# Regrouping the attention segments of a memory-augmented block: 20 tiles of three and 2 of two instead of 21 of three and one of one

## Chip, cores, metric

One core of a Trainium2 chip. The metric is the device time of one execution in microseconds (us). Most executions of one kernel agree within 0.3%, which here is about as large as the effect under study; the finer readings are therefore taken from traces, between fixed points of the program.

## The reference, cut to what matters

The output is `x + A(xn) + B(xn)` with `xn = layernorm(x)`, for 2048 tokens of width 1024. `B` is a mixer followed by an MLP. `A` cuts the tokens into 64 segments of 32, puts 8 memory rows before each, and runs attention with 32 heads of size 128 over the 40 rows. A segment's memory is the attention output at the memory rows of the segment before:

```
for s in range(n_seg):
    h = concat([mem, xs], axis=1)           # 8 memory rows, 32 tokens
    q, k, v = h @ Wq, h @ Wk, h @ Wv        # 32 heads of 128
    scores = where(mask, q @ k.T * scale, -1e9)
    o = softmax(scores) @ v @ Wo
    mem = o[:, :M]                          # memory of the next segment
    outs.append(o[:, M:])
```

## The kernel before

The kernel replaces the serial chain of memories by a closed form that it checks at the end (with a serial fallback that does not run here), so all segments can be computed at once. Each segment then needs 33 columns, 32 tokens and one memory column; the first tile has 7 more. Segments are packed into tiles, at most three to a tile, which is 99 rows of at most 128; a mask keeps the segments of a tile apart. Tiles are packed into five blocks. For each block and each group of four heads, the kernel projects the block's columns to Q and K (64 matmuls, whose moving operand is as wide as the block), then for each tile does four score matmuls, a softmax, a transpose by DMA, and four value matmuls. 64 = 21 x 3 + 1, so one tile held a single segment:

```python
def tiles_of(b):
    gis = list(range(4 * b, 4 * b + 4)) + ([21] if b == 3 else [20] if b == 4 else [])
    ...
        s = 1 if gi == 21 else 3            # segments in the tile
    ...
```

Blocks 0 to 4 had 4, 4, 4, 5 and 5 tiles and 403, 396, 396, 429 and 495 columns. The projection reads its columns as one run in blocks 0 and 3 ("flat"), and in blocks 1, 2 and 4 as strips of 99, each starting at a multiple of 104:

```python
if b == 3:
    rhs = lambda k: hTb[:, k, :nb]
else:
    rhs = lambda k: hTb[:, k, :].rearrange("p (t c) -> p t c", t=nt)[:, :, 0:99]
...
for k in range(KT):     # 8 matmuls, one PSUM bank
    nc.tensor.matmul(ps[:, :nb] ..., w[:, k, hh * P:(hh + 1) * P], B["rhs"](k), start=(k == 0), stop=(k == KT - 1))
```

The groups of a tile of T columns, for a group of four heads; the first operand of a matmul after the output is the stationary one, loaded as weights:

```python
for hh in range(4):     # scores: stationary 128 x T, moving 128 x T
    nc.tensor.matmul(S3[:, hh, :], QT[:, hh, c0:c0 + T], KTt[:, hh, c0:c0 + T], start=True, stop=True)
...                     # mask, exp, sum, scale, transpose
for hh in range(4):     # values: stationary T x 128, moving T x T
    nc.tensor.matmul(O3[:, hh, :], V[:T, t["i"], hh * P:(hh + 1) * P], PTr[:T, hh, :T], start=True, stop=True)
```

The score and value groups are issued between projections of eight matmuls each, so that TensorE always has work.

Of the kernel before, what the change touches and what calls it, by code (L numbers as in the profile page):

```python
# [15 lines left out]
BF16 = mybir.dt.bfloat16  # L16
# [7 lines left out]
P = 128  # L24
S = 2048
D = 1024
KT = D // P
# [3 lines left out]
H = 32  # L31
DH = 128
M = 8
SEG = 32
# [43 lines left out]
def kernel(  # L78
# [16 lines left out]
    nc = tc.nc  # L95
# [14 lines left out]
    R1_v = R1_d.rearrange("(n p) d -> p n d", p=P)  # L110
    xn_d = tc.dram_tile([S, D], BF16, name="xn_scratch")
    xn_v = xn_d.rearrange("(n p) d -> p n d", p=P)
    hT_d = {b: tc.dram_tile([P, KT * c], BF16, name=f"hT{b}_scratch") for b, c in ((1, 416), (2, 416), (3, 432), (4, 520))}
    V_d = tc.dram_tile([S, H * DH], BF16, name="V_scratch")
    Vr_d = tc.dram_tile([NQ + 1, H * DH], BF16, name="Vmem_scratch")

# [17 lines left out]
    eye9 = const_tile("c_eye9", np.concatenate([np.eye(M, dtype=np.float32), np.ones((M, 1), np.float32)], 1))  # L134
    mask_first = const_tile("c_mask_first", _tile_mask(3, True))
    mask_reg = const_tile("c_mask_reg", _tile_mask(3, False))
    mask_last = const_tile("c_mask_last", _tile_mask(1, False))
    GT = cpool.tile([P, KT, NQ], F32)
    MZ = cpool.tile([P, KT, NQ + 1], BF16)
    gthr = cpool.tile([1, NQ], F32)  # L140
# [15 lines left out]
    def row_norms(pool, ppool, tag, src, in_place=False):  # L156
# [6 lines left out]
        nc.tensor.matmul(ps[:1, :NQ], ones_f[:], sr[:], start=True, stop=True)  # L163
        return ps

    def tiles_of(b):
        gis = list(range(4 * b, 4 * b + 4)) + ([21] if b == 3 else [20] if b == 4 else [])
        out_, c = [], 0
        for i, gi in enumerate(gis):
            s = 1 if gi == 21 else 3  # L170
            first = b == 0 and i == 0
            nm = s + (M - 1 if first else 0)
            msk = mask_first if first else (mask_reg if s == 3 else mask_last)
            r0 = 0 if first else 7 + 3 * gi
            out_.append(dict(c0=c, ntok=s * SEG, nm=nm, T=s * SEG + nm, mask=msk, r0=r0, tok=i * 96, i=i, gi=gi))
            c += s * SEG + nm
        return out_, c

    def fill(hTb, tl, x_of):

        for t in tl:
            a = 96 * t["gi"]
            end = a + t["ntok"]
            while a < end:
                j, o = divmod(a, P)
                w = min(P - o, end - a)
                d = t["c0"] + a - 96 * t["gi"]
                nc.vector.tensor_copy(hTb[:, :, d:d + w], x_of(j)[:, :, o:o + w])
                a += w
            d = t["c0"] + t["ntok"]  # L190
            nc.vector.tensor_copy(hTb[:, :, d:d + t["nm"]], MZ[:, :, t["r0"]:t["r0"] + t["nm"]])

    with tc.manual_schedule(engines={mybir.EngineType.PE, mybir.EngineType.SP, mybir.EngineType.Pool}), ExitStack() as actx:
# [6 lines left out]
        with ExitStack() as bctx:  # L200
# [381 lines left out]
            for hg in range(8):  # L582
                cs_ = slice(hg * 512, (hg + 1) * 512)
                while len(wvs) < min(8, hg + 3):
                    load_wv()
                wv = wvs[hg]
                if 1 <= hg < 5:
                    nc.gpsimd.dma_start(wo_sb[:, (hg - 1) * 8:hg * 8, :], Wo_v[:, (hg - 1) * 8:hg * 8, :])
                for m4 in range(4):
                    Vs = vsp.tile([P, 4, 512], BF16, tag="Vs")  # L590
                    for j in range(4):
                        ps = psum.tile([P, 512], F32, tag="mm", bufs=4)
                        for k in range(KT):
                            nc.tensor.matmul(ps[:], xT[:, m4 * 4 + j, k, :], wv[:, k, :], start=(k == 0), stop=(k == KT - 1))  # L594
                        if j % 2 == 0:
                            nc.scalar.copy(Vs[:, j, :], ps[:])  # L596
                            if (hg, m4, j) == (7, 3, 2):
                                nc.scalar.activation(etab[:], ps[:, 0:1], ACTF.Exp, scale=0.0)
                        else:
                            nc.vector.tensor_copy(Vs[:, j, :], ps[:])  # L600
                    nc.sync.dma_start(V_d[m4 * 512:(m4 + 1) * 512, cs_].rearrange("(j p) c -> p j c", p=P), Vs[:])
                if hg == 1:
                    for t in pns:
                        nc.gpsimd.memset(t[:], 0.0)
                if 1 <= hg < 5:
                    b, (tl, nb) = hg, tiles_of(hg)
                    if b != 3:
                        for t in tl:
                            t["c0"] = 104 * t["i"]
                    hTs = abig.tile([P, KT, 432 if b == 3 else 104 * len(tl)], BF16, tag="oX", name=f"hTs{b}")  # L610
                    nc.gpsimd.memset(hTs[:], 0.0)
                    fill(hTs, tl, lambda j, b=b: xT[:, j])
                    nc.gpsimd.dma_start(hT_d[b][:], hTs[:].rearrange("p k c -> p (k c)"))
                if hg == 6:
                    first_w = [wtile(), wtile()]
                    for w, src in zip(first_w, (Wq_v, Wk_v)):
                        nc.sync.dma_start(w[:], src[:, :, 0:512])
                if hg == 7:
                    second_w = [wtile(), abig.tile([P, KT, 512], BF16, tag="oXb", name="wk1")]
                    for w, src in zip(second_w, (Wq_v, Wk_v)):  # L620
                        nc.sync.dma_start(w[:], src[:, :, 512:1024])
                if hg == 0:
                    tl, nb = tiles_of(0)
                    hTb0 = early.tile([P, KT, 408], BF16, tag="hTb0")
                    fill(hTb0, tl, lambda j: xT[:, j])
# [7 lines left out]
        def block_setup(b):  # L633
            tl, nb = tiles_of(b)
            ntok = sum(t["ntok"] for t in tl)
            if b == 0:
                hTb, rhs = hTb0, lambda k: hTb0[:, k, :nb]
            else:
                nt = len(tl)
                hTb = early.tile([P, KT, 432 if b == 3 else 104 * nt], BF16, tag=f"hTb{b % 2}")  # L640
                nc.gpsimd.dma_start(hTb[:].rearrange("p k c -> p (k c)"), hT_d[b][:])
                if b == 3:
                    rhs = lambda k: hTb[:, k, :nb]
                else:
                    rhs = lambda k: hTb[:, k, :].rearrange("p (t c) -> p t c", t=nt)[:, :, 0:99]
                    for t in tl:
                        t["c0"] = 104 * t["i"]
            return dict(b=b, tiles=tl, nb=nb, ntok=ntok, rhs=rhs, cols=nb if b in (0, 3) else 104 * len(tl))

        def load_values(B, V, hg):  # L650
            b, cs_ = B["b"], slice(hg * 512, (hg + 1) * 512)
            r, n = 384 * b, 5 if b == 4 else 4
            nc.sync.dma_start(V[0:96, 0:n, :], V_d[r:r + 96 * n, cs_].rearrange("(t p) c -> p t c", p=96))
            if b == 0:
                nc.sync.dma_start(V[96:106, 0, :], Vr_d[0:10, cs_])
                nc.sync.dma_start(V[96:99, 1:4, :], Vr_d[10:19, cs_].rearrange("(t j) c -> j t c", j=3))
            else:
                nc.sync.dma_start(V[96:99, 0:n, :], Vr_d[7 + 12 * b:7 + 12 * b + 3 * n, cs_].rearrange("(t j) c -> j t c", j=3))
            if b == 3:
                nc.sync.dma_start(V[0:32, 4, :], V_d[S - 32:S, cs_])  # L660
                nc.sync.dma_start(V[32:33, 4, :], Vr_d[70:71, cs_])

        def proj(B, w, hh, dst, scale):
            nb, nt = B["nb"], len(B["tiles"])
            flat = B["b"] in (0, 3)
            ps = psum.tile([P, 512], F32, tag="mm", bufs=4)
            for k in range(KT):
                nc.tensor.matmul(ps[:, :nb] if flat else ps[:, :nb].rearrange("p (t c) -> p t c", t=nt), w[:, k, hh * P:(hh + 1) * P], B["rhs"](k), start=(k == 0), stop=(k == KT - 1))  # L668
            if flat:
                o, i = dst[:, hh, :nb], ps[:, :nb]  # L670
            else:
                o, i = dst[:, hh, :].rearrange("p (t c) -> p t c", t=nt)[:, :, 0:99], ps[:, :nb].rearrange("p (t c) -> p t c", t=nt)
            if scale is None:
                nc.scalar.copy(o, i)  # L674
            else:
                nc.scalar.mul(o, i, scale)  # L676
# [37 lines left out]
        class Out:  # L714
# [4 lines left out]
            def piece(self, hg):  # L719
# [3 lines left out]
                    self.Rt = iop.tile([P, 512], F32, tag="Rt")  # L723
                    nc.gpsimd.dma_start(self.Rt[:, :self.w], R_v[:, self.gi, self.cc])
                for h in range(4 * hg, 4 * hg + 4):
                    nc.tensor.matmul(self.ps[:, :self.w], self.oX[self.gl // 3][:, h, self.gl % 3 * P:(self.gl % 3 + 1) * P], wo_sb[:, h, self.cc], start=(h == 0), stop=(h == H - 1))  # L726
                if hg == 7:
                    ot = iop.tile([P, 512], BF16, tag="ot")
                    if DEBUG_A:
# [45 lines left out]
        for gi_, group in enumerate(groups):  # L775
# [3 lines left out]
            for hg in range(8):  # L779
# [26 lines left out]
                for i, (B, t, QT, KTt, V) in enumerate(work):  # L806
                    due = clock[0] + 1.0 + i * step
                    if B["b"] not in oXs:
# [1 line left out]
                        if B["b"] == 3:  # L810
                            oXs[3].append(abig.tile([P, H, P], BF16, tag="oXb", name="oXb"))
                        oX_last = oXs[B["b"]]
                    j, at = divmod(480 if t["gi"] == 21 else t["tok"], 384)
                    oX = oXs[B["b"]][j]

                    def s_item(t=t, hg=hg, QT=QT, KTt=KTt, V=V, oX=oX, at=at, due=due, gi_=gi_):
                        PTr = scores(t, hg, QT, KTt)
# [4 lines left out]
                        smalls.append((clock[0] + (12.0 if gi_ == 0 else 10.0), ("O", gi_), o_item))  # L822
                        return 0.18
                    smalls.append((due, ("S", gi_), s_item))
            outs = [Out(oXs[B["b"]], 3 * B["b"] + gl, gl, ch * 512) for B in Bs for gl in range(4 if B["b"] == 4 else 3) for ch in range(2)]


        o = outs.pop()
# [184 lines left out]
```

## Time and profile before

| | before |
|---|---|
| median time | 1520.25 us (3 runs, 1520.1 to 1525.81) |
| span of the profiled run | 1518.8 us |
| TensorE (PE) busy | 99% |
| VectorE / ScalarE busy in blocks 3 and 4 | 47% / 46% |
| blocks 1 and 2 / blocks 3 and 4, from the trace | 278.04 us / 314.75 us |

The last row is measured between starts on PE: from the first row that the timeline labels with the width of block 1 (the eight matmuls before it are merged into a row of block 0) to the first projection of block 3, and from there to what follows the last projection of block 4.

From the page of the kernel before: busy time by engine, the granted clock in 40 slices, and the chain that ended last, by engine.

```profile
PE 1508.2 (99%) x9778; PEld 806.7 (53%) x9850; DVE 545.9 (36%) x1138; ACT 504.8 (33%) x1142; POOL 179.1 (12%) x248
...
PEclk9999999999999999999999999999999999999999
...
PE 97%; DMA 1%; issue 0%; ACT 0%; SPq 0%; DVE 0%
```

PE is busy, at full clock, and it is the chain. A busy PE is not a PE at its peak: matmuls overlap in the trace. So durations say little, and the spacing from one start to the next says what a group costs. The next view, who PE waited for (us in total, times, longest), shows that there is nothing to win from waits.

```profile
PE warm L334 <- DVE wz L328: 1.4, 1, 1.4
PE psO L707 <- DMA PT<-Pn: 0.4, 1, 0.4
...
PE ps L307 <- DMA w_sb<-in_B_w_dram: 0.3, 1, 0.3
PE pso L726 <- issue: 0.2, 1, 0.2
```

The last row is no wait: at that place four weight loads stand on record but only three matmuls, so one matmul record is missing. Waits shorter than the view lists can still be read from starts: at 1291.26 us, in block 4, a value group starts 0.11 us late.

Timeline of the kernel before, in block 3, around a score group of the one-segment tile. The columns are start in us, duration in us, engine (PE matmuls, PEld weight loads), line, operation, operands, count.

```profile
1227.08 1.62 PE L668 MATMUL ps<-hTb,wt 128*128 128x429 bf16 x8
1228.62 0.16 PEld L683 LDWEIGHTS <-QT 128*33 128x33 bf16 x4 [0.36 <-issue]
1228.62 0.27 PE L683 MATMUL psS<-KT,QT 128*33 128x33 bf16 x4
...
1228.82 1.20 PEld L668 LDWEIGHTS <-wt 128*128 128x128 bf16 x8
1228.82 1.63 PE L668 MATMUL ps<-hTb,wt 128*128 128x429 bf16 x8
1230.11 0.40 PEld L683 LDWEIGHTS <-QT 128*99 128x99 bf16 x4
1230.29 0.35 PE L683 MATMUL psS<-KT,QT 128*99 128x99 bf16 x4
```

Read it by starts. The first projection takes 1228.62 - 1227.08 = 1.54 us before the 33-wide group can start; one ahead of a 99-wide group takes 1230.29 - 1228.82 = 1.47 even here, and 1.45 elsewhere. The 33-wide group takes 0.20 us, more than the 0.187 of a 99-wide one that streams three times as many columns. The weight loads of the 99-wide group start 0.18 us ahead of its first matmul (1230.11 to 1230.29); those of the 33-wide group start with it, and so do those of the projection behind it (1228.82). So there is a loss at both ends. In the single starts, the first 33-wide matmul comes 0.09 us late and the first of the projection behind the group 0.08 us late.

Timeline of the kernel before: a run of 16 flat 429-column matmuls, a run of 16 in five strips of 99, and what follows each.

```profile
1208.63 3.07 PE L668 MATMUL ps<-hTb,wt 128*128 128x429 bf16 x16
1211.54 0.35 PE L683 MATMUL psS<-KT,QT 128*99 128x99 bf16 x4
...
1364.25 3.54 PE L668 MATMUL ps<-hTb,wt 128*128 128x495 bf16 x16
1367.63 0.35 PE L683 MATMUL psS<-KT,QT 128*99 128x99 bf16 x4
```

The spacing is 2.91/16 = 182 ns and 3.38/16 = 211 ns (typically 3.37). In this trace 512 columns take 216 ns and 128 take 56, so 384 more columns take 160 ns, which is 2.4 columns per ns. At that rate 429 and 495 columns are 178.8 and 206.3 ns, so the five strips of 99 carry a little more on top than the flat run does.

### The profile page before, as it was taken

The numbers are of one execution on the slowest core, as the hardware profiler recorded it, in microseconds if no ns is written. First come the engines' busy times: TensorE is split into PE (matmuls) and PEld (weight loads), VectorE is DVE, ScalarE is ACT, GpSimd is POOL, SyncE is SP. The second block draws the span as 40 slices with busy tenths as digits, with TensorE's granted clock in tenths as the row PEclk, the third lists the DMA queues.
The fourth block names the chain that finished last, engine by engine and source line by source line (L and its number), as shares of the span: only waits on it lengthen the run. The fifth ranks groups of instructions, "written<-read, shape, count | busy, mean of one in ns | idle before, by whom it ended". The sixth has DMA issues, their size and how long they took to land.

```text
span 1518.8 us, 24267 instructions
## 1 busy us (share of the span) xinstructions
PE 1508.2 (99%) x9778; PEld 806.7 (53%) x9850; DVE 545.9 (36%) x1138; ACT 504.8 (33%) x1142; POOL 179.1 (12%) x248
## 2 busy tenths in 40 slices
PE   9999999999999999999999999999999999999998
PEld 7844444445444444444466645654665555445555
DVE  8382230100110122212146614651663266416542
ACT  6533203013022011111256614650663266326630
POOL 5231020211111231100000010001000100010001
PEclk9999999999999999999999999999999999999999
DMA  8699762353355887532499948992997399728711
GB/s 287 153 272 318 217 177 91 133 201 112 125 169 145 194 284 254 189 133 70 139 239 253 239 117 188 247 238 81 227 239 189 119 223 203 197 76 208 175 45 54
DMA packets 303387, 274.20 MB, mean 181 GB/s; under 512 B 153787, under 2 KB 270032, under 8 KB 303016
## 3 DMA queue, kind: packets, MB, share of 16 engines
q1 hardware_dynamic: 281096, 189.92, 49.5%
q0 software_dynamic: 22032, 82.63, 15.8%
q8 instruction: 79, 1.29, 0.4%
q14 instruction: 36, 0.29, 0.1%
q10 hardware_dynamic: 144, 0.07, 0.0%
HBM read 190.98 MB, written 46.19 MB: 156 GB/s over the span
## 4 chain that ended last, share of the span: by engine, by line
PE 97%; DMA 1%; issue 0%; ACT 0%; SPq 0%; DVE 0%
PE ps L668 30%; PE pso L726 14%; PE ps L594 14%; PE ps L536 13%; PE ps L562 13%; PE ps L394 4%; PE ps L317 3%; PE psS L683 2%; PE psO L707 2%; PE ps L486 1%; PE ps L853 1%; DMA w_sb<-in_B_w_dram 1%; PE gps L465 0%; PE ps L451 0%; DMA wt<-in_A_Wq_dram 0%; DMA PT<-Pn 0%
## 5 line engine op out<-in xcount | busy, mean ns | idle before, releaser
L668 PE MATMUL ps<-hTb,wt 128*128 128x396 bf16 (+3 forms) x2528 | 500.4, 344 | 0.1
L668 PEld LDWEIGHTS <-wt 128*128 128x128 bf16 x2528 | 231.9, 97 | 167.6 <-DMA wt<-in_A_Wq_dram 0.5
L594 PE MATMUL ps<-wt,xT 128*128 128x512 bf16 x1003 | 220.1, 379 | 1.1
L726 PE MATMUL pso<-wo_sb,oX 128*128 128x512 bf16 x938 | 209.3, 379 | 1.2 <-issue 0.2
L536 PE MATMUL ps<-xn3T,w_sb 128*128 128x512 bf16 x896 | 196.2, 379 | 0.0
L562 PE MATMUL ps<-w_sb,h3T 128*128 128x512 bf16 x873 | 194.3, 379 | 1.2
L594 PEld LDWEIGHTS <-xT 128*128 128x128 bf16 x1024 | 100.0, 98 | 121.0
L537 ACT ACTIVATE h3T<-ps 128x512 bf16<-128x512 f32 x112 | 66.8, 597 | 290.4 <-PE ps L536 289.5
L726 PEld LDWEIGHTS <-oX 128*128 128x128 bf16 x960 | 92.5, 98 | 108.4
L674 ACT CAST KT<-ps 128x396 bf16<-128x396 f32 (+3 forms) x160 | 82.1, 513 | 186.9 <-PE ps L668 185.9
L562 PEld LDWEIGHTS <-h3T 128*128 128x128 bf16 x896 | 86.8, 98 | 103.5
L536 PEld LDWEIGHTS <-w_sb 128*128 128x128 bf16 x896 | 86.4, 98 | 102.3
L689 DVE TENSOR_REDUCE sums<-sm 99x4 f32<-99x396 f32 (+2 forms) x176 | 97.5, 554 | 113.7 <-ACT sm L687 113.7
L676 ACT ACTIVATE QT<-ps 128x396 bf16<-128x396 f32 (+3 forms) x160 | 84.1, 525 | 118.7 <-PE ps L668 102.8
L685 DVE TENSOR_TENSOR sm<-psS,c_mask_reg_sb 99x396 f32<-99x396 f32 x160 | 91.2, 570 | 85.3 <-PE psS L683 84.7
L596 ACT CAST Vs<-ps 128x512 bf16<-128x512 f32 x64 | 37.4, 585 | 233.2 <-PE ps L594 175.0
L687 ACT ACTIVATE sm<-sm 99x396 f32<-99x396 f32 (+2 forms) x176 | 92.7, 527 | 64.6 <-DVE sm L685 61.0
L600 DVE CAST Vs<-ps 128x512 bf16<-128x512 f32 x64 | 44.2, 691 | 170.1 <-PE ps L594 158.1
L695 DVE TENSOR_TENSOR Pn<-sm,rs 99x396 bf16<-99x396 f32 (+2 forms) x176 | 98.9, 562 | 8.2 <-DMA PT<-Pn 2.1
L563 DVE TENSOR_TENSOR R<-ps,R 128x512 f32<-128x512 f32 x32 | 22.0, 690 | 182.7 <-PE ps L562 173.4
L733 POOL DMA_DIRECT2D out_dram<-ot x30 | 16.3, 545 | 584.0 <-DVE ot L732 578.1
L732 DVE TENSOR_TENSOR ot<-pso,Rt 128x512 bf16<-128x512 f32 (+1 forms) x33 | 22.3, 675 | 172.1 <-PE pso L726 166.9
(124 smaller groups left out, 1068.9 us busy)
## 6 DMA issues: line engine op xcount, KB each, us to landing
wt<-in_A_Wq_dram SPq DMA_DIRECT2D x76, 512.0 KB
wt<-in_A_Wk_dram SPq DMA_DIRECT2D x76, 512.0 KB
wt<-in_A_Wv_dram POOLq DMA_DIRECT2D x24, 1024.0 KB, 6.5
V_scratch<-Vs SPq DMA_DIRECT2D x32, 512.0 KB
V<-V_scratch SPq DMA_DIRECT2D x32, 384.0 KB
R_scratch<-x POOLq DMA_DIRECT2D x16, 512.0 KB, 3.8
R<-R_scratch SPq DMA_DIRECT2D x16, 512.0 KB
R_scratch<-R POOLq DMA_DIRECT2D x16, 512.0 KB, 3.1
```

The lines of the kernel that those rows point to most:

```text
L536: nc.tensor.matmul(ps[:].rearrange("p (n t) -> p n t", t=P), w3_sb[:, k, f * P:(f + 1) * P], xn3T[tb][:, :, k, :], start=(k == 0), stop=(k ...
L537: nc.scalar.activation(h3T[:, f, :], ps[:], ACTF.Gelu_apprx_tanh)
L562: nc.tensor.matmul(ps[:], h3T[:, f, j * P:(j + 1) * P], w4_sb[:, f, ch * 512:(ch + 1) * 512], start=(f == 0), stop=(f == FT - 1))
L594: nc.tensor.matmul(ps[:], xT[:, m4 * 4 + j, k, :], wv[:, k, :], start=(k == 0), stop=(k == KT - 1))
L668: nc.tensor.matmul(ps[:, :nb] if flat else ps[:, :nb].rearrange("p (t c) -> p t c", t=nt), w[:, k, hh * P:(hh + 1) * P], B["rhs"](k), star ...
L674: nc.scalar.copy(o, i)
L676: nc.scalar.mul(o, i, scale)
L685: nc.vector.tensor_tensor(sm[:T, :, :T], S3, t["mask"][:].unsqueeze(1).to_broadcast((T, 4, T)), op=ALU.add)
L687: nc.scalar.activation(e[:T, :, :T], sm[:T, :, :T], ACTF.Exp, scale=LN2)
L689: nc.vector.tensor_reduce(ss, e[:T, :, :T], axis=AX.X, op=ALU.add)
L695: nc.vector.tensor_tensor(Pn[:T, :, :T], e[:T, :, :T], rs[:T, :].unsqueeze(2).to_broadcast((T, 4, T)), op=ALU.mult)
L726: nc.tensor.matmul(self.ps[:, :self.w], self.oX[self.gl // 3][:, h, self.gl % 3 * P:(self.gl % 3 + 1) * P], wo_sb[:, h, self.cc], start=(h ...
```

## The change

64 = 20 x 3 + 2 x 2: blocks of 12, 12, 12, 14 and 14 segments, the last two with four tiles of three and one of two. Blocks 3 and 4 both have 462 columns, both flat. Cut to its core:

```diff
+    SEGS = ((3,) * 4,) * 3 + ((3,) * 4 + (2,), (2,) + (3,) * 4)
     def tiles_of(b):
-        gis = list(range(4 * b, 4 * b + 4)) + ([21] if b == 3 else [20] if b == 4 else [])
...
-            s = 1 if gi == 21 else 3
...
+        for i, n in enumerate(SEGS[b]):
...
-                if b == 3:
+                if b > 2:
                     rhs = lambda k: hTb[:, k, :nb]
...
-            flat = B["b"] in (0, 3)
+            flat = B["b"] in (0, 3, 4)
```

The rest follows from it: the mask for two segments, the loads of values (two small DMAs more per head group in block 4), and where the outputs of the last blocks are put.

More of the change, by code (lines that the diff above doesn't have):

```diff
@@ L112 @@
     xn_v = xn_d.rearrange("(n p) d -> p n d", p=P)
-    hT_d = {b: tc.dram_tile([P, KT * c], BF16, name=f"hT{b}_scratch") for b, c in ((1, 416), (2, 416), (3, 432), (4, 520))}
+    hT_d = {b: tc.dram_tile([P, KT * c], BF16, name=f"hT{b}_scratch") for b, c in ((1, 416), (2, 416), (3, 464), (4, 464))}
     V_d = tc.dram_tile([S, H * DH], BF16, name="V_scratch")
@@ L136 @@
     mask_reg = const_tile("c_mask_reg", _tile_mask(3, False))
-    mask_last = const_tile("c_mask_last", _tile_mask(1, False))
+    mask_two = const_tile("c_mask_two", _tile_mask(2, False))
     GT = cpool.tile([P, KT, NQ], F32)
@@ L164, in row_norms @@
         return ps
+    SEGS = ((3,) * 4,) * 3 + ((3,) * 4 + (2,), (2,) + (3,) * 4)
     def tiles_of(b):
-        gis = list(range(4 * b, 4 * b + 4)) + ([21] if b == 3 else [20] if b == 4 else [])
-        out_, c = [], 0
-        for i, gi in enumerate(gis):
-            s = 1 if gi == 21 else 3
-            first = b == 0 and i == 0
-            nm = s + (M - 1 if first else 0)
-            msk = mask_first if first else (mask_reg if s == 3 else mask_last)
-            r0 = 0 if first else 7 + 3 * gi
-            out_.append(dict(c0=c, ntok=s * SEG, nm=nm, T=s * SEG + nm, mask=msk, r0=r0, tok=i * 96, i=i, gi=gi))
-            c += s * SEG + nm
+        out_, c, tok, seg = [], 0, 0, sum(map(sum, SEGS[:b]))
+        for i, n in enumerate(SEGS[b]):
+            first = seg == 0
+            nm = n + (M - 1 if first else 0)
+            msk = mask_first if first else mask_reg if n == 3 else mask_two
+            out_.append(dict(c0=c, ntok=n * SEG, nm=nm, T=n * SEG + nm, mask=msk, r0=0 if first else 7 + seg, tok=tok, seg=seg, i=i, gi=sum(map(len, SEGS[:b])) + i))
+            c += n * SEG + nm
+            tok += n * SEG
+            seg += n
         return out_, c
@@ L181, in fill @@
         for t in tl:
-            a = 96 * t["gi"]
+            a = SEG * t["seg"]
             end = a + t["ntok"]
@@ L186, in fill @@
                 w = min(P - o, end - a)
-                d = t["c0"] + a - 96 * t["gi"]
+                d = t["c0"] + a - SEG * t["seg"]
                 nc.vector.tensor_copy(hTb[:, :, d:d + w], x_of(j)[:, :, o:o + w])
@@ L606 @@
                     b, (tl, nb) = hg, tiles_of(hg)
-                    if b != 3:
+                    if b < 3:
                         for t in tl:
                             t["c0"] = 104 * t["i"]
-                    hTs = abig.tile([P, KT, 432 if b == 3 else 104 * len(tl)], BF16, tag="oX", name=f"hTs{b}")
+                    hTs = abig.tile([P, KT, 464 if b > 2 else 104 * len(tl)], BF16, tag="oX", name=f"hTs{b}")
                     nc.gpsimd.memset(hTs[:], 0.0)
@@ L639, in block_setup @@
                 nt = len(tl)
-                hTb = early.tile([P, KT, 432 if b == 3 else 104 * nt], BF16, tag=f"hTb{b % 2}")
+                hTb = early.tile([P, KT, 464 if b > 2 else 104 * nt], BF16, tag=f"hTb{b % 2}")
                 nc.gpsimd.dma_start(hTb[:].rearrange("p k c -> p (k c)"), hT_d[b][:])
-                if b == 3:
+                if b > 2:
                     rhs = lambda k: hTb[:, k, :nb]
@@ L647, in block_setup @@
                         t["c0"] = 104 * t["i"]
-            return dict(b=b, tiles=tl, nb=nb, ntok=ntok, rhs=rhs, cols=nb if b in (0, 3) else 104 * len(tl))
+            return dict(b=b, tiles=tl, nb=nb, ntok=ntok, rhs=rhs, cols=nb if b in (0, 3, 4) else 104 * len(tl))
         def load_values(B, V, hg):
             b, cs_ = B["b"], slice(hg * 512, (hg + 1) * 512)
-            r, n = 384 * b, 5 if b == 4 else 4
-            nc.sync.dma_start(V[0:96, 0:n, :], V_d[r:r + 96 * n, cs_].rearrange("(t p) c -> p t c", p=96))
-            if b == 0:
-                nc.sync.dma_start(V[96:106, 0, :], Vr_d[0:10, cs_])
-                nc.sync.dma_start(V[96:99, 1:4, :], Vr_d[10:19, cs_].rearrange("(t j) c -> j t c", j=3))
-            else:
-                nc.sync.dma_start(V[96:99, 0:n, :], Vr_d[7 + 12 * b:7 + 12 * b + 3 * n, cs_].rearrange("(t j) c -> j t c", j=3))
-            if b == 3:
-                nc.sync.dma_start(V[0:32, 4, :], V_d[S - 32:S, cs_])
-                nc.sync.dma_start(V[32:33, 4, :], Vr_d[70:71, cs_])
+            for n, i0 in ((3, int(b == 4)),) + (((2, 4 if b == 3 else 0),) if b > 2 else ()):
+                t, k = B["tiles"][i0], 4 if n == 3 else 1
+                r, w = SEG * t["seg"], SEG * n
+                nc.sync.dma_start(V[0:w, i0:i0 + k, :], V_d[r:r + w * k, cs_].rearrange("(t p) c -> p t c", p=w))
+                if b == 0:
+                    nc.sync.dma_start(V[96:106, 0, :], Vr_d[0:10, cs_])
+                    i0, k, t = 1, 3, B["tiles"][1]
+                nc.sync.dma_start(V[w:w + n, i0:i0 + k, :], Vr_d[t["r0"]:t["r0"] + n * k, cs_].rearrange("(t j) c -> j t c", j=n))
         def proj(B, w, hh, dst, scale):
             nb, nt = B["nb"], len(B["tiles"])
-            flat = B["b"] in (0, 3)
+            flat = B["b"] in (0, 3, 4)
             ps = psum.tile([P, 512], F32, tag="mm", bufs=4)
@@ L725, in piece @@
                 for h in range(4 * hg, 4 * hg + 4):
-                    nc.tensor.matmul(self.ps[:, :self.w], self.oX[self.gl // 3][:, h, self.gl % 3 * P:(self.gl % 3 + 1) * P], wo_sb[:, h, self.cc], start=(h == 0), stop=(h == H - 1))
+                    nc.tensor.matmul(self.ps[:, :self.w], self.oX[0][:, h, self.oX[1] + self.gl * P:self.oX[1] + (self.gl + 1) * P], wo_sb[:, h, self.cc], start=(h == 0), stop=(h == H - 1))
                 if hg == 7:
@@ L812 @@
                         oX_last = oXs[B["b"]]
-                    j, at = divmod(480 if t["gi"] == 21 else t["tok"], 384)
-                    oX = oXs[B["b"]][j]
+                    at = SEG * t["seg"] - 384 * B["b"]
+                    oX = oXs[B["b"]][0]
+                    if B["b"] == 3 and at == 384:
+                        oX, at = oXs[3][1], 0
+                    elif B["b"] == 4:
+                        oX, at = (oXs[4][1], at) if at < P else (oX, at - P)
                     def s_item(t=t, hg=hg, QT=QT, KTt=KTt, V=V, oX=oX, at=at, due=due, gi_=gi_):
@@ L824 @@
                     smalls.append((due, ("S", gi_), s_item))
-            outs = [Out(oXs[B["b"]], 3 * B["b"] + gl, gl, ch * 512) for B in Bs for gl in range(4 if B["b"] == 4 else 3) for ch in range(2)]
+            outs = []
+            for B in Bs:
+                for gl in range(4 if B["b"] == 4 else 3):
+                    src = (oXs[B["b"]][0], 0) if B["b"] < 4 else (oXs[4][0], -P) if gl else (oXs[4][1], 0)
+                    outs += [Out(src, 3 * B["b"] + gl, gl, ch * 512) for ch in range(2)]
         o = outs.pop()
```

## The prediction

> **What bounds the kernel.** TensorE. The page gives PE 1508.2 us of a 1518.8 us span (99%), the chain that ended last is 97% PE, and the clock row is 9 in all 40 slices. The list of waits finds about 3 us in which PE waited at all, 1.4 of them at the start. In the attention stage ACT and DVE are busy under 60% of each stretch. So only the start-to-start spacing of matmuls in PE's timeline counts; bytes, DMA issues and ACT or DVE work are free unless PE comes to wait for them.
>
> **What does not change.** Projection columns: 403+396+396+429+495 = 2119 before, 403+396+396+462+462 = 2119 after. 22 tiles, 176 score and 176 value groups, and the output projection stay. Value loads gain two small DMAs per head group in the last block, off the chain.
>
> **What changes on PE.**
>
> 1. Projections of blocks 3 and 4. Spacing from runs of 16 in the timeline: 429 columns, flat: 2.91 us, 182 ns each. 495 columns in five strips of 99: 3.37 us, 211 ns each. At 2.4 columns per ns that is 178.8 and 206.3, so the flat form adds 3 ns and the five-strip form nearly 5. After, both blocks are flat with 462 columns, 192.5 + 3 = 195.5 ns (estimate). 512 matmuls each: 201.2 us before, 200.2 after: minus 1.0 us.
>
> 2. The single-segment tile. A normal score group (99x99, four heads) takes 0.187 us start to start, a value group 0.179. The 33-wide ones take 0.20 and 0.19 though they stream a third of the columns; the projection in front of them takes 1.55 us instead of 1.45, and a group right behind one 0.23 instead of 0.19. Weight loads of 99-wide groups start 0.18 us ahead of their first matmul, those of 33-wide groups only with it. The Trainium skill, "TensorEngine Tiling (Array Packing)", section Key Properties, says that changing the tiling mode drains TensorE; 33 rows or columns would fit a 64-wide tile, 66 would not. The trace shows the lost 0.10 us and the late weight loads; that a mode change causes them is my inference. So this tile costs about 0.62 us per head group, against 0.366 for a three-segment tile.
>
>    A two-segment tile: 66/2.4 = 27.5 ns a matmul plus the 3.4 to 5.5 ns that 99-wide ones show over their column time: about 0.256 us per tile (the 71-column matmuls near the end run at 32.5 ns, in line). Per head group: 2 x 0.256 - 0.366 - 0.62 = -0.47 us, times 8: minus 3.8 us. If 66-wide groups stalled too (about 0.56 us per tile), this term would be about +1 us.
>
> All of it is on the critical path, as PE is never idle there. No compensating wait expected: value groups come some 10 us behind their scores, as before, and the tail is the same work.
>
> **Predicted: 1515.6 us**, range 1512.8 to 1519.8. Chances: faster by over 2% 0.01, within 2% 0.98, slower 0.01.
>
> **What would show it.** Right: weight loads of 66-wide groups start ahead of their matmuls; groups about 0.13 us start to start; no 0.10 us lost before them; 462-column projections at 195 to 196 ns; blocks 3 and 4 (1133 to 1448 us before) 4 to 5 us shorter; everything earlier unchanged. Wrong: a lost 0.1 us ahead of 66-wide groups, or new PE waits on the transposes of Pn or on value loads.
>
> **What would make it wrong.** A stall of 66-wide groups too; a value group in the shorter last block waiting for its transpose; run-to-run scatter (1520.1 to 1525.8 before), as large as the effect.

## The result and the profile after

The median after is 1514.98 us (6 runs, 1514.58 to 1517.16) against 1520.24 us before (6 runs, 1519.88 to 1525.81): 5.3 us less. The ratio is 0.996, with a 95% interval of 0.9944 to 0.9975; a ratio is the mean time of one kernel's fast runs over that of the other's of the same rounds, so not quite the ratio of the medians. By the mark of 2% the two are the same.

From the page of the kernel after, the lines shown of before:

```profile
PE 1502.8 (99%) x9778; PEld 807.9 (53%) x9850; DVE 545.2 (36%) x1138; ACT 504.1 (33%) x1142; POOL 178.9 (12%) x248
...
PEclk9999999999999999999999999999999999999999
...
PE 98%; DMA 1%; issue 0%; ACT 0%; DVE 0%; SPq 0%
```

PE has the same number of matmuls on record and is busy 5.4 us less. It still waits for hardly anything (waits on PE, kernel after):

```profile
PE warm L335 <- DVE wz L329: 1.4, 1, 1.4
...
PE psO L706 <- DMA PT<-Pn: 0.2, 1, 0.2
```

Timeline of the kernel after, in block 3, around a score group of a two-segment tile:

```profile
1214.44 1.73 PE L667 MATMUL ps<-hTb,wt 128*128 128x462 bf16 x8
1215.81 0.37 PEld L682 LDWEIGHTS <-QT 128*66 128x66 bf16 x4
1216.00 0.29 PE L682 MATMUL psS<-KT,QT 128*66 128x66 bf16 x4
...
1216.13 1.72 PE L667 MATMUL ps<-hTb,wt 128*128 128x462 bf16 x8
...
1217.69 0.34 PE L706 MATMUL psO<-PT,V 99*128 99x99 bf16 x4
```

Now the weight loads start 0.19 us ahead, the group takes 0.13 us, and the projection before it takes 1.56 us, as the one after it does: nothing is lost ahead of the small group.

Timeline of the kernel after: a run of 16 flat 462-column matmuls, and a value group of a two-segment tile.

```profile
1223.47 3.28 PE L667 MATMUL ps<-hTb,wt 128*128 128x462 bf16 x16
1226.59 0.28 PE L706 MATMUL psO<-PT,V 66*128 66x66 bf16 x4
1226.71 0.36 PE L682 MATMUL psS<-KT,QT 128*99 128x99 bf16 x4
```

That is 3.12/16 = 195 ns, and 0.12 us for the value group.

Where the time came from: blocks 1 and 2 took 278.05 us (278.04 before), blocks 3 and 4 309.60 us (314.75): 5.15 us less (5.08 from the start of block 3 to the last matmul of the program). The profiled spans differ by 6.1 us, but 1.0 us of that was gained before block 3 began (at 1132.45 us instead of 1133.46), in a part that the change does not touch. About half came in the first 12 us, where the kernel before waited 0.3 us for a weight DMA, and half with a value group of block 0 that waited 0.4 us for its transpose and then 0.2. That point scattered from run to run among kernels that do the same work up to it (1132.4 to 1138.3 us), so it is no effect of the change.

### The profile page after: what moved, and what is told of

It reads as the page before. It is cut to its first block, busy times and chain, and to the rows that moved or that the text cites. A ratio compares the mean times of both kernels' runs of the same rounds, so it can differ in the third digit from the quotient of the medians.

```text
span 1512.7 us, 24295 instructions
## 1 busy us (share of the span) xinstructions
PE 1502.8 (99%) x9778; PEld 807.9 (53%) x9850; DVE 545.2 (36%) x1138; ACT 504.1 (33%) x1142; POOL 178.9 (12%) x248
## 4 chain that ended last, share of the span: by engine, by line
PE 98%; DMA 1%; issue 0%; ACT 0%; DVE 0%; SPq 0%
PE ps L667 30%; PE pso L725 15%; PE ps L595 15%; PE ps L537 13%; PE ps L563 13%; PE ps L395 4%; PE ps L318 3%; PE psS L682 2%; PE psO L706 2%; PE ps L860 1%; PE ps L487 1%; PE gps L466 0%; PE ps L452 0%; DMA PT<-Pn 0%; DMA xt<-in_A_x_dram 0%
## 5 line engine op out<-in xcount | busy, mean ns | idle before, releaser
L667 PE MATMUL ps<-hTb,wt 128*128 128x396 bf16 (+2 forms) x2528 | 497.5, 343 | 0.0
L725 PE MATMUL pso<-wo_sb,oX 128*128 128x512 bf16 (+1 forms) x972 | 209.3, 372 | 1.1
L725 PEld LDWEIGHTS <-oX 128*128 128x128 bf16 x992 | 96.1, 98 | 106.5
L673 ACT CAST KT<-ps 128x462 bf16<-128x462 f32 (+2 forms) x160 | 81.9, 512 | 191.0 <-PE ps L667 189.2
L675 ACT ACTIVATE QT<-ps 128x462 bf16<-128x462 f32 (+2 forms) x160 | 83.9, 525 | 113.1 <-PE ps L667 101.5
L684 DVE TENSOR_TENSOR sm<-psS,c_mask_reg_sb 99x396 f32<-99x396 f32 x152 | 86.7, 570 | 76.9 <-PE psS L682 76.9
```

The lines of the kernel that those rows point to most:

```text
L667: nc.tensor.matmul(ps[:, :nb] if flat else ps[:, :nb].rearrange("p (t c) -> p t c", t=nt), w[:, k, hh * P:(hh + 1) * P], B["rhs"](k), star ...
L673: nc.scalar.copy(o, i)
L675: nc.scalar.mul(o, i, scale)
L684: nc.vector.tensor_tensor(sm[:T, :, :T], S3, t["mask"][:].unsqueeze(1).to_broadcast((T, 4, T)), op=ALU.add)
L725: nc.tensor.matmul(self.ps[:, :self.w], self.oX[0][:, h, self.oX[1] + self.gl * P:self.oX[1] + (self.gl + 1) * P], wo_sb[:, h, self.cc], s ...
```

## The experiments

Two theories of the one-segment tile had to be told apart. Mine: operands of up to 64 rows or columns put the array into another mode, and entering and leaving that mode costs the lost time, so the cost is there or not there, with a step above 64. The rival: groups so short simply cannot hide their weight loads, so that the loss fades with width. A third reading, that the width of the moving operand decides (it is narrow in both kinds of small group), is looked up in the trace of before. Besides, the change moved two things at once, the tile and the strips of the last block, so each had to be seen alone.

The lengths of blocks 3 and 4 in the profiles, and the medians of the timed rounds, beside before:

| run | blocks 3 and 4, us | minus before | median, us | before |
|---|---|---|---|---|
| before | 314.75 | | | |
| after | 309.60 | -5.15 | 1514.98 | 1520.24 |
| e1_flat4 | 313.77 | -0.98 | 1520.11 | 1520.79 |
| e2_w64 | 315.24 | +0.49 | 1520.69 | 1520.79 |
| e3_w65 | 312.88 | -1.87 | 1517.70 | 1520.79 |
| e9_w65 (the same again) | 311.81 | -2.94 | 1516.92 (one run) | 1520.51 |
| e4_w65s | 313.27 | -1.48 | 1518.50 | 1520.77 |
| e5_twice | 315.45 | +0.70 | 1520.92 | 1520.77 |
| e6_allflat | 309.77 | -4.98 | 1514.07 | 1520.79 |
| e7_after (after again) | 310.37 | -4.38 | 1515.09 | 1520.51 |
| e8_allflat (e6 again) | 309.57 | -5.18 | 1513.29 | 1520.51 |

All gave correct results, and all profiles were in the fast state, but for e9, a single run, whose state is unknown; it had clock 1.0.

### e1_flat4: the flat form alone

```diff
-                if b == 3:
+                if b > 2:
                     rhs = lambda k: hTb[:, k, :nb]
...
-            flat = B["b"] in (0, 3)
+            flat = B["b"] in (0, 3, 4)
```

> The kernel before, its tiles untouched, but the last block's 495 columns stored and projected as one flat run instead of five strips of 99. My theory: the 512 projection matmuls go from 211 to about 209.3 ns each (206.3 column time plus the 3 ns of the flat form), so the last block is 0.9 us shorter, and nothing else moves; the 33-wide tile still loses 0.10 us ahead of each of its groups. A rival, that the strips are nothing and the gain of the change is all from somewhere else: 0 us, 211 ns as before.

Timeline of e1_flat4, a run of 16 in the last block and what follows:

```profile
1365.13 3.51 PE L668 MATMUL ps<-hTb,wt 128*128 128x495 bf16 x16
1368.48 0.35 PE L683 MATMUL psS<-KT,QT 128*99 128x99 bf16 x4
```

3.35/16 = 209.4 ns instead of 211, and blocks 3 and 4 are 0.98 us shorter: the strips of 99 cost what I took them to cost. (0.11 us of the 0.98 is the late value group of before at 1291.26, which this profile does not have.) The projection ahead of a 33-wide group still takes 1.55 us. The ratio of times, 0.9991 (0.9973 to 1.0009), cannot resolve a microsecond; the trace can.

### e2_w64, e3_w65, e9_w65: the same tile, 64 and 65 wide

The one-segment tile is moved to the front of its block's columns, so that `T` can be set to 64 or 65 and take some of its neighbour's columns along; the mask and the copies keep them out of the result. The two kernels differ in `WIDE` alone.

```diff
+WIDE = 65          # 64 in e2_w64
...
-        out_, c = [], 0
+        out_, c = [], SEG + 1 if b == 3 else 0
...
-            out_.append(dict(c0=c, ntok=s * SEG, nm=nm, T=s * SEG + nm, ...))
+            out_.append(dict(c0=0 if gi == 21 else c, ntok=s * SEG, nm=nm, T=WIDE if gi == 21 else s * SEG + nm, ...))
...
+                nc.sync.dma_start(V[33:WIDE, 4, :], V_d[0:WIDE - 33, cs_])
```

> The kernel before, its tiles untouched, but the single-segment tile's score and value groups widened from 33 to 64 rows and columns by taking 31 of its neighbour's columns along, masked out; results stay right. Theory (a mode of the array for operands of up to 64 rows or columns, entered and left at a cost): 64 is still in that mode, so the 0.10 us ahead of each group stays, weight loads still start only with their matmuls, and the time is that of before, within 0.3 us. Rival (the cost comes of groups so short that their weight loads cannot be hidden, so it falls off with width): most of it is gone at 64, about 2.5 us faster.

> As the 64-wide run, but 65 wide: one row and column more. Theory: the stall is gone in one step; score and value groups take 0.125 to 0.13 us start to start with nothing lost before them, against about 0.62 us per head group for the two before: 8 x (0.62 - 0.255) = 2.9 us less than before, and than the 64-wide run. Rival (falls off with width): the same as the 64-wide run within 0.1 us.

> The 65-wide kernel again, for a second profile. In the first, blocks 3 and 4 were 1.9 us shorter than before, not 2.9, with two waits of value groups for their transposes (0.31 and 0.44 us) near the boundary of blocks 3 and 4. If those waits were chance, they are gone and the stretch is 2.6 to 2.9 us shorter than before; if the 65-wide tile brings them, they come back at the same place.

Timeline of e2_w64 around a 64-wide score group:

```profile
1232.08 1.62 PE L677 MATMUL ps<-hTb,wt 128*128 128x429 bf16 x8
1233.63 0.20 PEld L692 LDWEIGHTS <-QT 128*64 128x64 bf16 x4 [0.35 <-issue]
1233.63 0.31 PE L692 MATMUL psS<-KT,QT 128*64 128x64 bf16 x4
...
1233.88 1.63 PE L677 MATMUL ps<-hTb,wt 128*128 128x429 bf16 x8
```

Timeline of e9_w65 around a 65-wide one:

```profile
1225.42 1.62 PE L677 MATMUL ps<-hTb,wt 128*128 128x429 bf16 x8
1226.69 0.36 PEld L692 LDWEIGHTS <-QT 128*65 128x65 bf16 x4
1226.87 0.29 PE L692 MATMUL psS<-KT,QT 128*65 128x65 bf16 x4
...
1227.00 1.62 PE L677 MATMUL ps<-hTb,wt 128*128 128x429 bf16 x8
```

One column decides. At 64, the weight loads start with their matmuls, the projection before takes 1.55 us, and the group 0.25. At 65, the loads start 0.18 us ahead, the projection takes 1.45, and the group 0.13: more columns in half the time. The rival, a loss that fades with width, falls. The timed rounds agree: the ratio to before is 0.9972 (0.9955 to 0.9990) at 65, and 0.9995 (0.9977 to 1.0012) at 64.

`T` sets the moving width too, so these runs alone leave open which operand decides. The kernel before has matmuls that tell: groups of 32 with a full 128x128 stationary operand and only 64 moving columns. Timeline of the kernel before, in `B`; each 512-column row stands for 56 matmuls (56 weight loads; of the second row's, 54 are on record), the first with its columns in four strips of 128, the second flat:

```profile
260.09 12.25 PE L536 MATMUL ps<-xn3T,w_sb 128*128 128x512 bf16 x56
272.18 1.10 PE L451 MATMUL ps<-xb,wt 128*128 128x64 bf16 x32
273.11 12.25 PE L562 MATMUL ps<-w_sb,h3T 128*128 128x512 bf16 x54
285.20 1.10 PE L451 MATMUL ps<-xb,wt 128*128 128x64 bf16 x32
```

The 64-column matmuls are 0.93/32 = 29 ns apart, and the 512-column ones take 12.09/56 = 216 ns, the last before the narrow group included: nothing is lost at either end. The other way round, a matmul with 71 moving columns but a stationary operand of one column (fp32, L163, in both places of the program where one follows a 512-column matmul) starts 0.309 us after the 512-column matmul ahead of it, instead of 0.216: the same 0.09 us. So a narrow moving operand is not enough, and what decides lies in the stationary operand, its columns or its rows (for few rows with a wide moving operand, no run has a case).

The 64-wide run was not quite the time of before that I had expected within 0.3 us: its blocks 3 and 4 are 0.49 us longer, since its score groups take 0.25 us and not 0.20, and its value groups 0.22 and not 0.19 (8 x 0.08 = 0.6, less the 0.11 us by which a value group of before was late). The median shows no difference.

The first profile of the 65-wide kernel gave only 1.87 us of the 2.9 expected. Timeline of e3_w65, at the boundary of blocks 3 and 4:

```profile
1282.62 0.34 PE L716 MATMUL psO<-PT,V 99*128 99x99 bf16 x4 [0.31 <-DMA PT<-Pn]
...
1289.02 0.34 PE L716 MATMUL psO<-PT,V 99*128 99x99 bf16 x4 [0.44 <-DMA PT<-Pn]
```

Two value groups waited for their transposes; PE sat idle for 0.75 us, and by starts the groups came 0.48 and 0.60 us late, 1.08 in all. In the second profile of the same kernel those waits were gone and the stretch was 1.07 us shorter than in the first and 2.94 us shorter than before, so the waits are chance and they are the whole shortfall. Two such waits (0.60 and 0.22 us by starts, 0.43 us of idle time shown for the first) also came up in the second profile of after, whose stretch was 310.37 us instead of 309.60. This is the scatter to keep in mind for one profile: about 1 us.

### e4_w65s: the scores alone widened

```diff
# e3_w65, but the value groups as before
-            T, nt = t["T"], t["ntok"]
+            T, nt = t["ntok"] + t["nm"], t["ntok"]
```

> As the 65-wide run, but only the scores are widened (stationary operand of 65 columns); the value groups stay 33 rows deep. Theory: only the score groups lose their stall; 8 x (0.10 + 0.20 - 0.13) = 1.4 us less than before, while the projection ahead of each value group still takes 0.10 us more. If the stall came from rows (depth) alone: 0 us.

Timeline of e4_w65s, a value group of 33 rows and, later, a score group of 65 columns, each with the projection before it:

```profile
1222.49 1.62 PE L676 MATMUL ps<-hTb,wt 128*128 128x429 bf16 x8
1224.05 0.26 PE L715 MATMUL psO<-PT,V 33*128 33x33 bf16 x4
...
1226.10 1.62 PE L676 MATMUL ps<-hTb,wt 128*128 128x429 bf16 x8
1227.55 0.29 PE L691 MATMUL psS<-KT,QT 128*65 128x65 bf16 x4
```

1.56 us ahead of the 33-row group, 1.45 ahead of the 65-column one; 1.48 us less than before, with 1.4 expected. The columns of the score groups and the rows of the value groups each bear about half of the cost (1.48, and 2.94 - 1.48 = 1.46 us; the 0.11 us late value group of before is in the first number, so 1.37 is fairer).

### e5_twice: the small score group twice in a row

```diff
-            for hh in range(4):
+            for hh in (0, 1, 2, 3) * (2 if t["gi"] == 21 else 1):
                 nc.tensor.matmul(S3[:, hh, :], QT[...], KTt[...], start=True, stop=True)
```

> The kernel before with the four 33-wide score matmuls issued twice in a row (the same result). Theory (the cost is in entering and leaving the mode, not per matmul): the second four cost only their own spacing, some 25 to 32 ns each, so 0.10 to 0.13 us per head group, 8 x that = 0.8 to 1.0 us more than before. Rival (each small group, or each small matmul, pays): 0.2 us (at the 50 ns each that 0.20 us for four comes to, 1.6 us in all) up to 0.30 us per head group (2.4 us in all).

Timeline of e5_twice:

```profile
1227.42 1.62 PE L668 MATMUL ps<-hTb,wt 128*128 128x429 bf16 x8
1228.97 0.37 PE L683 MATMUL psS<-KT,QT 128*33 128x33 bf16 x8
1229.27 1.63 PE L668 MATMUL ps<-hTb,wt 128*128 128x429 bf16 x8
```

Eight matmuls take 0.30 us where four took 0.20, and the loss ahead stays (1228.97 - 1227.42 = 1.55 us). So four more cost 0.10 us, some 25 ns each, and the rest, about 0.09 us ahead of the group and 0.08 us between it and what follows, is paid once per visit, however many small matmuls it has. The stretch grew by 0.70 us; 8 x 0.10 = 0.8 less the 0.11 us of the late value group of before, which this profile does not have, comes to that. That each small matmul pays (1.6 us), or each group (2.4 us), is refuted.

### e6_allflat, e7_after, e8_allflat: all blocks flat

The kernel after, with blocks 1 and 2 flat too:

```diff
-                if b > 2:
-                    rhs = lambda k: hTb[:, k, :nb]
-                else:
-                    rhs = lambda k: hTb[:, k, :].rearrange("p (t c) -> p t c", t=nt)[:, :, 0:99]
-                    for t in tl:
-                        t["c0"] = 104 * t["i"]
+                rhs = lambda k: hTb[:, k, :nb]
...
-            flat = B["b"] in (0, 3, 4)
+            flat = True
```

> The kernel after, with blocks 1 and 2 also stored and projected flat (396 columns in one run instead of four strips of 99). Theory: 1024 matmuls go from 169.2 to about 168 ns (165 column time plus 3), so 1.0 to 1.2 us less than after: about 1513.9 us against before's 1520.2. Rival (strips cost nothing; 462-column projections are cheaper only by chance): equal to after.

> The kernel after, unchanged, as the reference for the next run on the same chip: 1515 us, 5.2 us under before; the stretch from the first projection of block 3 to the end of the last one 309.6 us as in its first profile, if that is not luck.

> The all-flat kernel again, beside after on one chip. The first profile had its blocks 1 and 2 1.7 us shorter, so I expect about 1.7 us less than after in the traces and in the medians; the rival, that the 0.9 us between the medians of two different calls was scatter, expects equality.

Timeline of e8_allflat, 16 projections of block 1 and what follows:

```profile
857.82 2.84 PE L659 MATMUL ps<-hTb,wt 128*128 128x396 bf16 x16
860.50 0.34 PE L698 MATMUL psO<-PT,V 99*128 99x99 bf16 x4
```

The same of the kernel before, in four strips:

```profile
858.49 2.87 PE L668 MATMUL ps<-hTb,wt 128*128 128x396 bf16 x16
861.20 0.34 PE L707 MATMUL psO<-PT,V 99*128 99x99 bf16 x4
```

2.68/16 = 167.5 ns against 2.71/16 = 169.4. Blocks 1 and 2 took 276.33 us in both profiles, 1.72 us less than before and after (278.04 and 278.05); I had expected 1.0 to 1.2. Beside after the medians are 1513.29 (1513.12 to 1514.29) and 1515.09 us (1514.65 to 1515.34). The ranges do not overlap, and the 1.8 us between the medians agrees with the trace.

Is it the strips as such? The traces say no. Four strips of 128 took 12.09/56 = 216 ns in the view of `B` above, the same as 512 columns flat. What fits every width here is that a run or strip with an odd number of columns costs as much as one with a column more, plus 2.5 ns for each matmul (mean spacing in long runs, without the highest and lowest twentieth):

| columns | measured, ns | all runs made even, / 2.4 + 2.5 |
|---|---|---|
| 396 flat (e8) | 167.5 | 167.5 |
| 4 x 99 (before) | 169.2 | 400: 169.2 |
| 429 flat (before) | 181.7 | 430: 181.7 |
| 462 flat (after) | 195.0 | 195.0 |
| 495 flat (e1) | 209.1 | 496: 209.2 |
| 5 x 99 (before) | 210.9 | 500: 210.8 |
| 512 flat, and 4 x 128 (before) | 215.8 | 215.8 |

71 and 72 columns also take the same, 32.5 and 32.4 ns. This is a rule read off the widths; no run was made to test it.

This version beats both kernels: its ratio to before was 0.9955 in both calls (0.9936 to 0.9974, 0.9941 to 0.9968).

## Why the prediction was right

- *PE bounds, and nothing else counts.* Right. The added DMAs and the changed work of VectorE and ScalarE left no new kind of wait; the single short waits for a transpose come and go between profiles of one kernel.
- *Everything before block 3 unchanged.* Right for blocks 1 and 2 (278.04 and 278.05 us). The profiled span shows 1.0 us more gain than that stretch explains; that is scatter in the start and in block 0.
- *Term 1, projections: minus 1.0 us.* Right in kind, a little small. 462 columns took 195.0 ns, not 195.5, so 512 x (181.9 + 210.6 - 2 x 195.0) ns = about 1.3 us. The 3 ns on top were taken from 429 columns, an odd number; 462, an even one, carries 2.5. e1 showed the flat form alone: 0.98 us, 0.9 without the late group of before.
- *Term 2, the small tile: minus 3.8 us.* Right. The 66-wide groups took 0.13 and 0.12 us with nothing lost before them (0.256 for both predicted). What is left of the 5.15 us after term 1 is about 3.9 us. The small tile cost about 0.60 us per head group by single starts, not quite the 0.62 of the prediction.
- *The mechanism*, marked as an inference: supported. The loss is there at 33 and at 64 and gone at 65; it comes with either the columns (scores) or the rows (values) of the stationary operand, and not with a narrow moving operand alone; and it is paid per visit, not per matmul. What the runs show is the step and the cost per visit. A drain of the array would fit what the Trainium skill says ("TensorEngine Tiling (Array Packing)", Key Properties: "Changing tiling mode (not just tile) drains the TensorE"), but the traces do not show that a mode changes here, so this part stays an inference.
- *The sum:* 1515.6 us predicted, 1514.98 measured. That is closer than the scatter of one profile (about 1 us) lets anyone aim; the terms are what was right, and the last half microsecond is luck.

So the gain did not come from the better balance of the blocks as such: the number of projected columns is 2119 in both. About three quarters came from no longer having operands of 33 rows or columns, one quarter from the widths: some 0.9 us from one flat run instead of five strips of 99, some 0.4 us (by the rule above, not tested alone) from 462 columns being an even number where 429 and 495 are odd.

## What to carry to other kernels

On an engine that never waits, cost a change by the spacing from start to start in the timeline, not by durations or by counted work: a tile of a third of the size cost 0.60 us per head group against 0.37 for a full one. When a remainder tile would give the stationary operand 64 rows or columns or fewer in the middle of full-size matmuls, spread the remainder over two tiles above 64, or pad it to 65: padding alone was worth 2.9 us here, the split with its flat blocks 5.2. Avoid moving operands made of strips of an odd width: one run of 396 instead of four strips of 99 was worth 1.7 us for 1024 matmuls, while strips of 128 cost nothing.

## What the Trainium skill lacked or had wrong

- "TensorEngine Tiling (Array Packing)", Key Properties, states the drain without its cost, and nowhere that ordinary matmuls fall under it by their shape alone. Here plain matmuls with a 33- or 64-wide operand, with no tiling asked for, lost 0.09 us ahead of each group of four and about as much again before what followed it; at 65 wide nothing was lost. That this loss is the drain is not shown.
- "TensorE: Matmul & The Clock Gate", Back-to-back issue gap: the formula N/2.4 + 2.5 ns held for flat operands of even width (462 columns: 195.0 ns both ways; 396: 167.5 both ways); an odd width took 0.4 ns more (429: 181.7 against 181.25). The lower sustained figure given there for N = 512, about 131 ns, did not show: 12 output-projection matmuls of 512 columns in the kernel after took 2.59 us, 216 ns each. Nor did the 81 ns for N = 128: 128-column matmuls in `B` of the kernel before (L317), each with its own weights, ran at 56 ns.
- No page gives the cost of a moving operand in strips or of odd width. Four strips of 99 cost 1.9 ns per matmul over one run of 396 (169.4 against 167.5), five strips some 1.6 ns over one run of 495 (211 against 209.4); four strips of 128 cost nothing over 512 flat (216 ns both).
- "TensorE: Matmul & The Clock Gate", Part 3: Packing small matmuls, under The mechanism, says that weight loads overlap with matmuls in flight only where the row group differs, while it also speaks of a background weight buffer. Here the loads of 66- to 99-wide groups are recorded 0.18 to 0.19 us ahead of their matmuls, during projections that use all 128 rows; only the first loads of groups of 64 and less, and of what follows such a group, were not.
- The floor of about 25 ns between starts for small N in the same page (Wait — 56ns, not 53.3ns?) is neither lacking nor wrong: four added 33-wide matmuls took 0.10 us in e5_twice.
